# Six visits of four banks, or three of six: regrouping attention inside a fused attention and FFN kernel

## The chip, the cores and the metric

The kernel runs on one core of one Trainium2 chip. The metric is device time in microseconds (us) of that core. A run here is one execution with its own time. In an experiment the profiled execution is its first run; that of the kernel before is one more execution, of 569.2 us, at the long end of the four timed ones. A profiled span is mostly about 1.8 us shorter than the time of the same run. With a single core no second state was seen: every run with a timed comparison counted as fast. Runs without a comparison (e1, e2 and e5 to e9, one execution each) have no known state; of these I rest on the trace, and give the time for the record.

## The reference

Linformer attention over 8 batches of 8 heads, and then a gated feed-forward network (FFN) over the 8192 tokens:

```python
k_proj = np.einsum('ks,bhsd->bhkd', E, k)        # 1024 keys -> 64
v_proj = np.einsum('ks,bhsd->bhkd', F, v)
scores = scale * np.matmul(q, k_proj.transpose(0, 1, 3, 2))
attn   = np.exp(scores - max); attn = attn / (sum(attn) + 1e-09)
out    = np.matmul(attn, v_proj)                 # 64 per head
x      = out.transpose(0, 2, 1, 3).reshape(8192, 512)
gate   = 1.0 / (1.0 + np.exp(-(x @ w_gate)))     # 512 x 1536
val    = x @ w_val                               # 512 x 1536
return (gate * val @ w_out)                      # 1536 x 512
```

(The maximum and the sum are shortened here.) The FFN is most of the work: 288 matmuls of 128x128 weights on 512 columns per batch, against 56 small matmuls of attention that run side by side in parts of the array.

## The kernel before

TensorE runs the FFN of batch b in 32 steps (24 of "G and V", 8 output projections), and at fixed steps it is interrupted for a piece of the attention of batch b+1. I call such an interruption a visit. Helpers add an instruction to a plan with what it reads, writes and which PSUM bank it holds; the plan makes the semaphores. There are eight banks: four in turn for the FFN (`ffn`), four for attention (`att`).

One FFN step and its gate, which hold two banks:

```python
def mstep(blk, m):
    pbs = {n: ffn.next() for n in "GV"}
    for n in "GV":
        for i in range(NI):                    # 4 matmuls each
            mm_one(blk, m, i, n, pbs[n])       # 128x128 weights, 512 columns
    gate(blk, m, pbs["G"], pbs["V"])           # ScalarE tanh -> sig, VectorE (sig+1)*V -> hT
```

The attention of batches 2 to 7 (cut to its core):

```python
def kv():                                      # 16 matmuls in pairs, tiles 128*64, one bank
    ...                                        # then ScalarE: bank -> kpd, vpD
def turn_kd(): ...                             # DMA transpose kpd -> kpD
def sc(r2):                                    # tiles 64*64
    for r in (2 * r2, 2 * r2 + 1):
        bks = [att.next(), att.next()]
        ...                                    # 4 matmuls kpD, qT -> two banks
        ...                                    # ScalarE exp -> eT, frees the banks
def den():                                     # 8 matmuls in fours, tiles 128*32, one bank
    ...
    for c in range(4):
        rec(c, bk)                             # VectorE reciprocal, 128 columns each
def gather(): ...                              # DMA rden -> rrow
def spread(rnd): ...                           # GpSimd partition_broadcast rrow -> rb
def xo(r2):                                    # tiles 64*64
    for r in (2 * r2, 2 * r2 + 1):
        bks = [att.next(), att.next()]
        ...                                    # 4 matmuls vpD, eT -> two banks
        for g in range(2):                     # VectorE: bank * rb -> xT, frees the bank
            dve(... tensor_tensor(xT[...], bank[...], rb[...], ALU.mult) ...)

return [kv, turn_kd, lambda: sc(0), lambda: sc(1), den, gather,
        lambda: spread(0), lambda: spread(1), lambda: xo(0), lambda: xo(1)]
# at steps
spots = (3, 6, 10, 13, 16, 16, 20, 23, 26, 29)
```

So six of these pieces are visits of TensorE: projection, two of scores, denominators, two of outputs. Batch 1 has its own list, with the division spread by matmul: four reciprocals, a split of the result into two bf16 parts (`split`: a copy to `rhi`, the rest to `rhl`), and broadcast matmuls on `rhl` (`bc`). Batch 0 comes first of all, in two halves, while the loads arrive; I call the time until the FFN runs without gaps the head. In it, idle time of TensorE is filled with dummy matmuls (`busy(n)`), and GpSimd issues the loads, one after the other, each costing it some 0.8 to 1.0 us.

The softmax here doesn't subtract the row's maximum and nothing guards it: scores larger than these inputs give would overflow.

## Time and profile before

| | before |
|---|---|
| median of all its runs beside the change | 568.76 us (567.77 to 569.41, 4 runs) |
| profiled span | 567.4 us |
| TensorE busy | 97% |
| FFN matmuls without a gap, each | 0.2158 us |
| attention visits of batches 2 to 7 | 36, each 0.23 us beside its matmuls |
| period per batch | 67.41 us |

How to read the profile: "PE" is TensorE, "PEld" its weight loads, DVE VectorE, ACT ScalarE, POOL GpSimd. A line of the timeline has start, duration, engine, line of the program, operation, what it writes and reads, shapes, and how many instructions are merged; in brackets the idle time before it and who ended it. The durations of matmuls include their way through the array, so I never add them: what a stretch costs is read from the starts on both sides of it.

VectorE's timeline in the head, where the first half of batch 0 is divided:

```profile
16.94 0.95 DVE L593 RECIPROCAL rden<-pF 64x128 f32<-64x128 f32 x1 [0.55 <-PE pF L220]
17.92 0.22 DVE L594 CAST rhi<-rden 64x128 bf16<-64x128 f32 x1
...
18.94 0.96 DVE L593 RECIPROCAL rden<-pA 64x128 f32<-64x128 f32 x1 [0.42 <-PE pA L220]
19.93 0.62 DVE L594 CAST rhi<-rden 64x128 bf16<-64x128 f32 x1
```

GpSimd's timeline, the issue of a load for the second batch:

```profile
19.48 1.02 POOL L238 DMA_DIRECT2D KV<-in_v_dram  x1
```

The view of one tile, `rb`, the broadcast reciprocals: minimum, median and maximum duration in ns, and first and last start.

```profile
L829 POOL PARTITION_BROADCAST rb<-rrow x96: 792/797/802, 130.4 to 479.2; - x96
L854 DVE TENSOR_TENSOR xT<-pA,rb x56: 680/681/684, 81.9 to 489.8; 128x512 bf16<-128x512 f32 x56
```

In the kernel before, broadcasts and multiplies are regular to within 10 ns.

### The profile page before, as it was taken

How to read it: one execution, taken by the hardware profiler on the slowest of the kernel's cores; microseconds unless marked ns; L12 is line 12 of the kernel's file. 1: busy time of each engine (PE TensorE's matmuls, PEld its weight loads, DVE VectorE, ACT ScalarE, POOL GpSimd, SP SyncE). 2: the span in 40 equal slices, each digit the busy share in tenths (PEclk: the TensorE clock that was granted, in tenths of full speed). 3: DMA queues.
4: the chain of work that ended last, by engine and by line, in shares of the span. 5: the costliest groups of instructions: out<-in, count | busy, mean ns of one | idle time of the engine just before them, and what ended most of it. 6: DMA issues, size and time to landing. Idle time of an engine off the chain costs nothing.

```text
span 567.4 us, 7629 instructions
## 1 busy us (share of the span) xinstructions
PE 550.5 (97%) x2963; PEld 247.0 (44%) x3018; DVE 249.5 (44%) x397; ACT 177.4 (31%) x314; POOL 107.2 (19%) x148
## 2 busy tenths in 40 slices
PE   5899999999999999999999999999999999999998
PEld 4444434444444444444444444444444444444444
DVE  4544464353623545235443256334462354633332
ACT  2644632432143322352223422243214332222220
POOL 9400201007200080002600054000700007000000
PEclk9999999999999999999999999999999999999999
DMA  9999999936944059512677046560601001010112
GB/s 162 198 201 201 140 212 167 208 79 115 146 84 96 21 113 183 93 47 62 117 141 121 24 105 107 121 103 37 114 18 48 37 22 39 37 37 20 38 38 92
DMA packets 76564, 56.00 MB, mean 99 GB/s; under 512 B 34704, under 2 KB 68240, under 8 KB 76528
## 3 DMA queue, kind: packets, MB, share of 16 engines
q0 software_dynamic: 33984, 29.89, 34.8%
q1 hardware_dynamic: 42544, 25.63, 18.1%
q8 instruction: 23, 0.38, 0.3%
q14 instruction: 13, 0.11, 0.1%
HBM read 60.29 MB, written 16.78 MB: 136 GB/s over the span
## 4 chain that ended last, share of the span: by engine, by line
PE 95%; DVE 1%; DMA 1%; issue 1%; ACT 0%; POOL 0%; DVEq 0%; POOLq 0%
PE pF L220 88%; PE pA L220 7%; DMA KV<-in_k_dram 1%; DVE xT L645 1%; DVE hT L940 0%; DVE rden L783 0%; DVE rhl L794 0%; ACT qT L224 0%; DVE rhi L792 0%; POOL quad L313 0%; DVE ost L971 0%; DVEq L102 0%; POOLq L1116 0%
## 5 line engine op out<-in xcount | busy, mean ns | idle before, releaser
L940 DVE SCALAR_TENSOR_TENSOR hT<-sig,pF 128x512 bf16<-128x512 f32 x192 | 130.8, 685 | 200.0 <-PE pF L220 145.1
L224 ACT ACTIVATE sig<-pF 128x512 f32<-128x512 f32 x192 | 114.4, 599 | 318.3 <-PE pF L220 315.9
L220 PE MATMUL pF<-xT,wV 128*128 128x512 bf16 x753 | 196.2, 379 | 1.1 <-DVE hT L940 0.3
L220 PE MATMUL pF<-xT,wG 128*128 128x512 bf16 x746 | 194.4, 379 | 2.8 <-issue 1.3
L220 PE MATMUL pF<-wO,hT 128*128 128x512 bf16 (+2 forms) x762 | 173.9, 376 | 1.5 <-issue 0.8
L220 PEld LDWEIGHTS pF<-wO,hT 128*128 128x128 bf16 x780 | 74.7, 98 | 92.6 <-issue 6.2
L220 PEld LDWEIGHTS pF<-xT,wV 128*128 128x128 bf16 x768 | 75.1, 98 | 91.1 <-DVE hT L940 0.8
L220 PEld LDWEIGHTS pF<-xT,wG 128*128 128x128 bf16 x768 | 72.2, 98 | 95.3 <-issue 12.3
L829 POOL PARTITION_BROADCAST rb<-rrow x96 | 70.7, 798 | 217.1 <-DMA rrow<-rden 212.0
L971 DVE TENSOR_SCALAR ost<-pF 128x512 f32<-128x512 f32 (+1 forms) x65 | 44.4, 684 | 103.5 <-PE pF L220 103.4
L224 ACT ACTIVATE eT<-pA 128x512 bf16<-128x512 f32 x63 | 32.7, 606 | 8.4 <-PE pA L220 8.4
L854 DVE TENSOR_TENSOR xT<-pA,rb 128x512 bf16<-128x512 f32 x56 | 34.7, 682 | 0.0
L783 DVE RECIPROCAL rden<-pA 128x128 f32<-128x128 f32 x28 | 24.1, 916 | 0.0
L238 POOL DMA_DIRECT2D KV<-in_v_dram x9 | 7.8, 872 | 83.9 <-PE pF L220 83.9
L220 PE MATMUL pA<-KV,EFT 128*64 128x512 bf16 (+2 forms) x168 | 16.0, 332 | 1.0 <-DMA KV<-in_k_dram 1.0
L224 ACT ACTIVATE kpd<-pA 64x1024 bf16<-64x1024 f32 x6 | 6.1, 1017 | 28.3 <-PE pA L220 28.3
L238 POOL DMA_DIRECT2D KV<-in_k_dram x9 | 8.0, 889 | 32.3 <-PE pF L220 32.2
L220 PEld LDWEIGHTS pA<-KV,EFT 128*64 128x64 bf16 x168 | 8.3, 115 | 8.6 <-issue 3.4
L224 ACT ACTIVATE vpD<-pA 64x512 bf16<-64x512 f32 (+2 forms) x22 | 10.2, 465 | 2.2 <-PE pA L220 1.7
L220 PE MATMUL pA<-qT,kpD 64*64 64x512 bf16 (+1 forms) x140 | 10.4, 367 | 0.0
L220 PE MATMUL pA<-eT,vpD 64*64 64x512 bf16 (+1 forms) x140 | 10.4, 367 | 0.0
L238 POOL DMA_DIRECT2D Qb<-in_q_dram x11 | 9.4, 865 | 0.0
(69 smaller groups left out, 89.5 us busy)
## 6 DMA issues: line engine op xcount, KB each, us to landing
out_dram<-ost SPq DMA_DIRECT2D x63, 256.0 KB, 2.1
Qb<-in_q_dram POOLq DMA_DIRECT2D x7, 1024.0 KB, 15.6
KV<-in_k_dram POOLq DMA_DIRECT2D x7, 1024.0 KB, 11.0
KV<-in_v_dram POOLq DMA_DIRECT2D x7, 1024.0 KB, 10.5
wO<-in_moe_w_out_dram POOLq DMA_DIRECT2D x1, 1536.0 KB, 12.0
wG<-in_moe_w_gate_dram POOLq DMA_DIRECT2D x5, 256.0 KB, 18.4
wV<-in_moe_w_val_dram POOLq DMA_DIRECT2D x5, 256.0 KB, 19.0
KV<-in_k_dram POOLq DMA_DIRECT2D x2, 512.0 KB, 8.8
```

Of the source, the lines that this page charges most:

```text
L220: return add("PE", lambda e: e.matmul(o, lhsT, rhs, **kw), r=r, x=[("bank", b)])
L224: return add("ACT", lambda e: e.activation(o, i, func, scale=scale), r=r, w=w, x=x)
L238: add("POOL", lambda e: e.dma_start(o, i), r=r, w=w, dma=sem)
L645: lambda e, g=g, o=o: e.tensor_tensor(o, bank[bks[g]][:, :].rearrange("p (r c) -> p r c", r=2), rb[:, 2 * R + g, :].rearrange("p (r c) -> ...
L783: lambda e: e.reciprocal(rden[:, cc], bank[bk][:, cc]),
L829: lambda e, n=n, i=2 * rnd + c, j=j, parts=parts: e.partition_broadcast(rb[0:parts, n, :], rrow[32 * j : 32 * j + 1, i, :], channels=parts),
L854: lambda e, r=r, g=g, n=n, bk=bks[g]: e.tensor_tensor(xT[s][:, r, :, 256 * g : 256 * g + 256], bank[bk][:, :].rearrange("p (f c) -> p f c" ...
L940: lambda e: e.scalar_tensor_tensor(hT[blk % 2][:, m, :], sg[:, :], 1.0, bank[pv][:, :], ALU.add, ALU.mult,),
L971: lambda e, pb=pb, c0=c0, c1=c1: e.tensor_scalar(o[:, c0:c1], bank[pb][:, 0 : c1 - c0], 0.5, None, op0=ALU.mult),
```

## The change

The intent: fewer interruptions of the FFN. A visit may hold six banks, four of attention and two borrowed from the FFN. So that the outputs' banks come free without waiting for the division, ScalarE copies them unscaled to SBUF (`xu`), and VectorE multiplies from there later. The third visit also projects the next batch's keys and values and forms the denominators. The core of the diff, cut:

```diff
-        Qb = [sbuf(f"Qb{i}", [P, H, S // P * DH], BF16) for i in range(2)]
+        Qb = sbuf("Qb", [P, H, S // P * DH], BF16)
...
+        xu = sbuf("xu", [P, 8, 512], FP32)
...
+            def scores():
+                f, a0, a1 = two(ffn), two(att), two(att)
+                for r, bks in ((2, f), (0, a0), (1, a1)):
+                    sc_one(r, bks)
+                exp_one(2, f)
+                exp_one(0, a0)
+                held["sc"] = a1
+
+            def mixed():
+                f, a0, a1 = two(ffn), two(att), two(att)
+                sc_one(3, f)
+                xo_one(0, a0)
+                xo_one(1, a1)
+                exp_one(3, f)
+                keep_x(0, a0)
+                held["x"] = a1
+
+            def outputs():
+                f, a0 = two(ffn), two(att)
+                xo_one(2, f)
+                xo_one(3, a0)
+                held["x"] = a0
+                if b + 1 < B:
+                    held["kv"] = att.next()
+                    kv(b + 1, held["kv"])
+                den()
+                keep_x(2, f)
+                rec(0)
...
-                spots = (3, 6, 10, 13, 16, 16, 20, 23, 26, 29)
+                spots = (3, 4, 6, 7, 12, 13, 14, 15, 15, 21, 23, 25, 27)
```

The second batch keeps its pieces, but their order and steps change:

```diff
-                    v_alone,
                     lambda: sc(0),
                     lambda: sc(1),
...
+                    v_alone,
+                    lambda: rec(3),
                     split,
...
-                spots = (12, 13, 14, 15, 16, 17, 18, 19, 20, 20, 21, 22, 23, 24)
+                spots = (12, 13, 14, 15, 16, 17, 18, 18, 19, 19, 21, 22, 23, 24)
```

Not shown: batch 2 has its own projection visit and its own steps, and the loads of the later batches are issued at other steps, with the queries last. And in the head there are more fillers, scores before denominators, another order of banks, and the loads of the second batch are written later:

```diff
-        busy(6)
+        busy(18)
...
-        den(0)
         sc(1)
+        den(0)
...
-        load_q(1)
-        load_k(1)
-        load_v(1)
+        def second_loads():
+            load_q(1)
+            load_k(1)
+            load_v(1)
...
+                put(5, second_loads)
```

## The prediction

> **What bounds the kernel now**
>
> I read the page first: engine shares, then the chain that ended last.
>
> ```profile
> PE 550.5 (97%) x2963; PEld 247.0 (44%) x3018; DVE 249.5 (44%) x397; ACT 177.4 (31%) x314; POOL 107.2 (19%) x148
> ...
> PE 95%; DVE 1%; DMA 1%; issue 1%; ACT 0%; POOL 0%; DVEq 0%; POOLq 0%
> ```
>
> TensorE is busy for 97% of the span and carries 95% of the chain; no other engine passes 44%. So only what shortens TensorE's own stream, or one of its few waits, can count. A busy share hides what lies between instructions, so next I read the TensorE timeline of the steady part, start by start.
>
> ```profile
> 230.29 1.92 PE L220 MATMUL pA<-KV,EFT 128*64 128x512 bf16 x16
> ...
> 289.84 1.03 PE L220 MATMUL pF<-xT,wG 128*128 128x512 bf16 x4
> ...
> 295.02 2.75 PE L220 MATMUL pF<-wO,hT 128*128 128x512 bf16 x12
> 297.70 1.92 PE L220 MATMUL pA<-KV,EFT 128*64 128x512 bf16 x16
> ```
>
> From 289.84 to 295.02 lie 24 feed-forward (FFN) matmuls without a gap: 5.18/24 = 0.2158 us each. Key projections follow each other at 67.41 us: that is one batch. Its FFN is 288 matmuls, 288 x 0.2158 = 62.15 us, so attention costs 5.26 us of TensorE per batch. The small attention matmuls run side by side in parts of the array, in "rounds" that cost one matmul's time: 8 rounds of projection (16 matmuls in pairs), 4 of scores, 2 of denominators, 4 of outputs: 18 x 0.2158 = 3.88 us. The other 1.38 us is what six interruptions of the FFN ("visits") cost: 0.23 us each. One visit seen directly:
>
> ```profile
> 311.65 1.03 PE L220 MATMUL pF<-xT,wV 128*128 128x512 bf16 x4
> 312.61 0.63 PE L220 MATMUL pA<-qT,kpD 64*64 64x512 bf16 x8
> 313.17 2.76 PE L220 MATMUL pF<-wO,hT 128*128 128x512 bf16 x12
> ```
>
> 311.65 + 4 x 0.2158 = 312.51, so the visit enters 0.10 us late; its two rounds end at 313.04 and the FFN resumes at 313.17, another 0.13. Nothing waits for an engine here: the price belongs to the change of tiling (128*128 to 64*64 and back).
>
> Then I looked for real waits of TensorE. The largest is in the second batch's attention:
>
> ```profile
> 72.88 1.03 PE L220 MATMUL pF<-xT,wV 128*128 128x512 bf16 x4
> 75.15 0.39 PE L220 MATMUL pA<-rhl,bsel 32*128 32x512 bf16 x4 [1.24 <-DVE rhl L794]
> ```
>
> 72.88 + 0.86 + 0.10 = 73.84 is when the visit could start; it starts 1.31 us later. The VectorE timeline says why:
>
> ```profile
> 72.89 0.95 DVE L783 RECIPROCAL rden<-pA 128x128 f32<-128x128 f32 x1
> 73.88 0.43 DVE L792 CAST rhi<-rden 128x512 bf16<-128x512 f32 x1
> 74.34 0.75 DVE L794 SCALAR_TENSOR_TENSOR rhl<-rhi,rows,rden 128x512 bf16<-128x512 bf16 x1
> ```
>
> The last reciprocal and the split sit in the very step before the broadcast needs them. Last, the head, from the same TensorE timeline:
>
> ```profile
> 9.35 1.06 PE L220 MATMUL pA<-KV,EFT 128*64 128x128 bf16 x16 [1.01 <-DMA KV<-in_k_dram]
> ...
> 13.24 1.03 PE L220 MATMUL pA<-ident,Qb 128*128 128x128 bf16 x8
> 14.21 0.30 PE L220 MATMUL pF<-ident,kp 128*64 128x128 bf16 x4
> ...
> 15.20 0.40 PE L220 MATMUL pA<-ident,Qb 128*128 128x128 bf16 x4
> 15.44 0.39 PE L220 MATMUL pF<-ident,Qb 128*128 128x128 bf16 x4
> ```
>
> Eight transposes take 0.97 us at 13.24 (0.12 each) and four take 0.24 at 15.20 (0.06 each): the array runs at half speed until about 14.5. But the arrival of data also paces it. Issue times plus times to landing give 11.8 for the second half of the keys, 13.2 and 14.5 for the queries, 17.0 and 19.7 for the values; each piece of TensorE work starts close behind its landing. The first FFN matmul is at 22.62.
>
> **What the Trainium skill says**
>
> "TensorEngine Tiling (Array Packing)", Key Properties: changing the tiling mode, not just the tile, drains TensorE. The trace agrees: 0.10 + 0.13 us per visit.
>
> "TensorE: Matmul & The Clock Gate", What's actually happening: the array runs at half clock until some 3.4 us of sustained work. The 0.12 and 0.06 us above agree.
>
> "VectorE: DVE Perf Modes", TRN2 errata: an fp32 tensor_tensor with SBUF operands takes (N+151)/0.96, 691 ns at 512. The trace has 682 ns for the present multiply, which reads PSUM, so the multiply's new source should cost nothing.
>
> "SBUF — State Buffer", Who interferes with whom: a VectorE instruction with two SBUF inputs contends with a GpSimd instruction that reads SBUF. The new multiply is one and the partition broadcast the other. No such overlap exists in the kernel before.
>
> **The change, part by part**
>
> *Visits.* The kernel before makes 6 x 6 = 36 visits for batches 2 to 7. The new one makes 18, and one more for batch 2's own key and value projection: 19. The rounds stay 18 per batch. Saved: 17 x 0.23 = 3.9 us. The third visit, however, changes tiling inside: 64*64 for outputs, 128*64 for the next projection, 128*32 for denominators. That is two inner changes for five batches and one for the last, 11 in all. Their size I take from the head, where projection changes straight to denominators:
>
> ```profile
> 17.92 0.22 PE L220 MATMUL pF<-KV,EFT 128*64 128x128 bf16 x1
> 18.07 0.83 PE L220 MATMUL pA<-eT,dsel 128*32 128x128 bf16 x8
> ```
>
> 17.92 + 0.05 for that matmul leaves 0.10 us. 11 x 0.10 = 1.1 us is given back: net -2.8 us.
>
> *Second batch.* The denominators move one step earlier and the value projection between the reciprocals, so about two more FFN steps of 1.73 us lie between split and broadcast. The 1.31 us wait should vanish: -1.3 us. The visits there stay ten.
>
> *Head.* More filler matmuls warm the array before the keys land; 18 cold ones (some 1.9 us from 7.5) may delay the first projection by 0.1 us, while later transposes and projections halve. The landings above cap the gain. Following VectorE, the first reciprocal stays at about 16.9, but the second need no longer wait 0.42 us for TensorE, so the first scaled outputs and the FFN start move up 0.4 to 0.5 us. I count -0.45.
>
> *Off the path.* ScalarE takes 8 more evictions per batch, 6 x 8 x 0.5 = 24 us over the run at 31% busy. VectorE's multiplies only change source. One query buffer instead of two makes the second batch's query load wait for the last transposes of the first, near 34.6; the weights ahead of it occupy the queue until the last lands at 17.0 + 21.4 = 38.4, so it arrives no later (43.4).
>
> Sum: -2.8 - 1.3 - 0.45 = -4.55. 568.17 - 4.55 = **563.6 us**.
>
> **Rivals**
>
> *Bank waits.* Each visit now borrows two of the FFN's four banks. The tightest place is the second visit after two FFN steps. Count from the first visit: its exponentials start 0.5 us in and four take 2.06, so the next tanh ends near 3.1 us; two more exponentials; the tanh after them ends near 4.6, and the gate on VectorE (0.69) frees the bank near 5.4. The second visit needs it at about 6.15. Slack 0.75 us: no wait, but it is the thinnest point. If ScalarE ran later by 1 us, six batches would lose some 0.3 us each, and the time would be about 565.5.
>
> *VectorE against GpSimd.* Broadcasts take 12.7 us per batch and start 10.3 us after the third visit; the first two multiplies (17 and 22 us after it) may overlap them. Each VectorE instruction could lose up to one broadcast, 0.8 us. Gates would slip by 1 to 2 us; the output projection beside them gives slack. I expect at most some tenths per batch; the bad case is 566.
>
> *Inner changes cost nothing, or double.* Nothing: 562.5. A full 0.23 each: 565.0.
>
> *The freed time is lost to loads.* Against it: TensorE waits for no load after 10 us, and the new loads are issued earlier.
>
> **Range and chances**
>
> The visit count and the 1.31 us wait are firm; inner changes, head and bank slack each move the sum by about a microsecond, mostly upward. 562.0 to 566.0 should hold it 8 times in 10. A 2% gain needs 11.4 us, more than all visits and stalls named here: 0.01. A 2% loss needs a wait of about 2 us in every batch: 0.01. Within 2%: 0.98.
>
> **What would show it**
>
> In the new TensorE timeline: period per batch of 62.15 + 3.88 + 3 x 0.23 + 0.2 = 66.9 us against 67.41; no wait for the split near 73 us; first FFN matmul near 22.2. Inner gaps of 0.1 between the three tilings. Wrong would be FFN matmuls marked as waiting for ACT eT, DVE hT or DVE xT after a visit, multiplies well over 0.69 us, or a broadcast over 0.8 us.

## The result, and the profile after

| | before | after |
|---|---|---|
| median | 568.76 us | 564.57 us (564.34 to 564.6, 4 runs) |
| profiled span | 567.4 us | 562.8 us |
| third FFN step starts | 26.66 us | 25.89 us |
| first broadcast matmul of batch 1 | 75.15 us | 73.07 us |
| period per batch | 67.41 us | 66.97 us |

The ratio of the times is 0.9927, with a 95% interval of 0.9909 to 0.9945. A ratio here is the mean time of one kernel's fast runs over that of the other's of the same rounds, so not quite the ratio of the medians. The change is worth 0.7%, within the 2% that counts as the same.

From the page of the kernel after, the engines' shares and the chain of work that ended last:

```profile
PE 551.9 (98%) x3032; PEld 248.8 (44%) x3032; DVE 258.5 (46%) x397; ACT 200.8 (36%) x362; POOL 113.0 (20%) x148
...
PE 96%; DMA 2%; DVE 1%; POOL 0%; issue 0%; ACT 0%; POOLq 0%
```

TensorE was the bound before and still is. ScalarE's 48 new copies made it 23 us busier, from 177.4 to 200.8, and VectorE went from 249.5 to 258.5 with as many instructions as before.

The TensorE timeline after, at the first visits of two batches and at one third visit:

```profile
162.31 0.41 PE L221 MATMUL pF<-qT,kpD 64*64 64x512 bf16 x4
...
180.38 1.03 PE L221 MATMUL pF<-xT,wV 128*128 128x512 bf16 x4
181.34 0.41 PE L221 MATMUL pF<-eT,vpD 64*64 64x512 bf16 x4
181.57 0.39 PE L221 MATMUL pA<-eT,vpD 64*64 64x512 bf16 x4
181.89 1.92 PE L221 MATMUL pA<-KV,EFT 128*64 128x512 bf16 x16
183.74 0.61 PE L221 MATMUL pA<-eT,dsel 128*32 128x512 bf16 x8
184.29 1.04 PE L221 MATMUL pF<-xT,wG 128*128 128x512 bf16 x4
...
229.28 0.41 PE L221 MATMUL pF<-qT,kpD 64*64 64x512 bf16 x4
```

The period is 229.28 - 162.31 = 66.97. In the third visit, the last FFN matmul gives way at 180.38 + 0.86 = 181.24; the visit starts 0.10 later. Four matmuls of 64*64 cost one round, two rounds would end at 181.34 + 0.43 = 181.77; the projection starts at 181.89, 0.12 later. Its eight rounds end at 183.62; the denominators start 0.12 later. Their two rounds end at 184.17, and the FFN resumes 0.12 later. Other third visits of the trace give 0.12 to 0.13 for each inner change. I use 0.125.

The broadcast matmuls of batch 1, where the kernel before waited 1.24 us:

```profile
72.11 1.03 PE L221 MATMUL pF<-xT,wV 128*128 128x512 bf16 x4
73.07 0.39 PE L221 MATMUL pA<-rhl,bsel 32*128 32x512 bf16 x4
```

72.11 + 0.86 + 0.10 = 73.07: no wait at all.

VectorE's and GpSimd's timelines in the head of the kernel after, which answer to those shown of before:

```profile
16.96 0.95 DVE L593 RECIPROCAL rden<-pF 64x128 f32<-64x128 f32 x1 [0.86 <-PE pF L221]
17.94 0.22 DVE L594 CAST rhi<-rden 64x128 bf16<-64x128 f32 x1
...
18.57 0.96 DVE L593 RECIPROCAL rden<-pA 64x128 f32<-64x128 f32 x1
19.57 0.23 DVE L594 CAST rhi<-rden 64x128 bf16<-64x128 f32 x1
```

```profile
17.00 0.87 POOL L239 DMA_DIRECT2D wV<-in_moe_w_val_dram  x1
```

The second reciprocal no longer waits (18.57 against 18.94, with the same start of the first), the second copy takes 0.23 us and not 0.62, and the load shown is GpSimd's last before the copies are done.

The view of tile `rb` after:

```profile
L831 POOL PARTITION_BROADCAST rb<-rrow x96: 792/797/1210, 137.1 to 473.0; - x96
L862 DVE TENSOR_TENSOR xT<-xu,rb x48: 678/684/1153, 143.2 to 481.2; 128x512 bf16<-128x512 f32 x48
```

Some multiplies and some broadcasts take half as long again or more: the contention that the prediction named as a rival, and two of its signs of being wrong. On the page the multiplies' mean went from 682 to 856 ns.

Three stretches make up the gain between these two traces. Until the third FFN step: 26.66 - 25.89 = 0.77. From there to the broadcast matmuls: 75.15 - 73.07 = 2.08 in all, so 1.31. From there to the end: 567.4 - 562.8 = 4.6 in all, so 2.5.

The theory at this point: fewer visits save 2.5, the vanished wait 1.31, a better head about 0.8. The rivals: that the head's share is chance, since loads land differently from run to run; that the gap of a visit belongs to interruption as such and not to the change of tiling; that the contention or the banks cost something that hides in the sum.

### The profile page after: what moved, and what is told of

It reads as the page before. It is cut to its first block, busy times and chain, and to the rows that moved or that the text cites. A ratio compares the mean times of both kernels' runs of the same rounds, so it can differ in the third digit from the quotient of the medians.

```text
span 562.8 us, 7706 instructions
## 1 busy us (share of the span) xinstructions
PE 551.9 (98%) x3032; PEld 248.8 (44%) x3032; DVE 258.5 (46%) x397; ACT 200.8 (36%) x362; POOL 113.0 (20%) x148
## 4 chain that ended last, share of the span: by engine, by line
PE 96%; DMA 2%; DVE 1%; POOL 0%; issue 0%; ACT 0%; POOLq 0%
PE pF L221 90%; PE pA L221 6%; DMA Qb<-in_q_dram 2%; DVE xT L645 1%; POOL KV L239 0%; DVE hT L992 0%; DVE rden L593 0%; ACT qT L225 0%; POOL quad L313 0%; DVE rhl L596 0%; DVE ost L1023 0%; DVE rhi L594 0%; POOLq L1179 0%
## 5 line engine op out<-in xcount | busy, mean ns | idle before, releaser
L221 PE MATMUL pF<-xT,wG 128*128 128x512 bf16 x768 | 198.0, 379 | 1.2 <-DVE xT L645 1.2
L221 PE MATMUL pF<-wO,hT 128*128 128x512 bf16 (+1 forms) x780 | 175.7, 376 | 0.0
L831 POOL PARTITION_BROADCAST rb<-rrow x96 | 77.0, 862 | 286.3 <-DMA rrow<-rden 281.1
L862 DVE TENSOR_TENSOR xT<-xu,rb 128x512 bf16<-128x512 f32 x48 | 39.2, 856 | 0.0
L785 DVE RECIPROCAL rden<-pA 128x128 f32<-128x128 f32 x28 | 26.6, 951 | 12.3 <-PE pA L221 12.3
L225 ACT ACTIVATE eT<-pA 128x512 bf16<-128x512 f32 x39 | 21.3, 626 | 1.6 <-PE pA L221 1.6
L225 ACT ACTIVATE eT<-pF 128x512 bf16<-128x512 f32 x25 | 13.6, 595 | 22.6 <-PE pF L221 22.4
L225 ACT ACTIVATE xu<-pA 128x512 f32<-128x512 f32 x36 | 19.1, 617 | 0.0
L225 ACT ACTIVATE rb<-pA 128x512 f32<-128x512 f32 x14 | 7.4, 601 | 2.1 <-PE pA L221 2.1
```

Of the source, the lines that this page charges most:

```text
L221: return add("PE", lambda e: e.matmul(o, lhsT, rhs, **kw), r=r, x=[("bank", b)])
L225: return add("ACT", lambda e: e.activation(o, i, func, scale=scale), r=r, w=w, x=x)
L785: lambda e: e.reciprocal(rden[:, cc], bank[bk][:, cc]),
L831: lambda e, n=n, i=2 * rnd + c, j=j, parts=parts: e.partition_broadcast(rb[0:parts, n, :], rrow[32 * j : 32 * j + 1, i, :], channels=parts),
L862: lambda e, r=r, g=g, n=n, x=x: e.tensor_tensor(xT[s][:, r, :, 256 * g : 256 * g + 256], x.rearrange("p (f c) -> p f c", f=2), rb[:, n, :] ...
```

## The experiments

There were twelve runs of kernels. e1 to e4 were on one chip, e5 to e8 on a second, e9 and e10 on the first again, e11 and e12 on a third, each time with runs of the kernel before (a single one beside e5 to e8). All twelve gave correct results.

### One part at a time

**The late loads alone** (e1), on the kernel before:

```diff
-        load_q(1)
-        load_k(1)
-        load_v(1)
+        def second_loads():
+            load_q(1)
+            load_k(1)
+            load_v(1)
...
+                put(5, second_loads)
```

> The kernel before with one edit: the loads of the second batch (queries, keys, values, output weights) are issued after the sixth FFN step, as in the changed kernel, instead of ahead of the FFN. In the kernel before, the copy that splits the second reciprocal ran 0.62 us from 19.93 while GpSimd issued the value load (19.48 to 20.50); in the changed kernel it ran 0.23 us. Theory 'loads': GpSimd's issue work slows that copy, so here the copy takes about 0.23 us and the first FFN matmul moves from 22.62 to about 22.2; the steady FFN from 26.66 to about 26.3. Rival 'order and fillers': the copy was slow for another reason; it stays near 0.6 and the first FFN matmul stays at 22.6. The end of the span should move by the same 0.3 to 0.4 us or not at all.

Measured: 569.22 us, span 567.4. The experiment failed. The loads were written later, but each engine has its own order, GpSimd had nothing in between, and nothing made the loads wait: in the trace they are issued at 17.73, 18.61 and 19.47, as before. In the kernel after, they wait because the single query buffer must be free. So this run is a repeat of the kernel before. It is of use as such: here the two copies take 0.70 and 0.34 us, where the kernel before had 0.22 and 0.62.

**The head alone** (e2): fillers, order and banks of the kernel after, on the kernel before; the loads stay early.

```diff
-        busy(6)
+        busy(18)
...
-        den(0)
         sc(1)
+        den(0)
```

> The kernel before with the head of the changed kernel alone: more filler matmuls, second scores ahead of the first denominators, the new turn of banks; the loads stay early. Theory 'loads plus order': of the 0.77 us that the changed kernel gains by its third FFN step, order and fillers give about 0.4 (the second reciprocal starts near 18.57 instead of 18.94), and the copy stays slow at about 0.6 us: third FFN step near 26.3 instead of 26.66. Rival 'order and fillers alone': the whole 0.77, 25.9.

Measured: 568.32 us, span 566.5. The third FFN step starts at 25.79, the copies take 0.22 and 0.25, and the wait of batch 1 is still there (1.24 us at 74.27). By its place alone this third FFN step says little, since e3 below reaches 25.78 with the old head; the count from the first reciprocal, under "The head", shows that order and fillers shorten the head even with early loads.

**The second batch alone** (e3), on the kernel before, 5 rounds:

```diff
-                    v_alone,
                     lambda: sc(0),
...
+                    v_alone,
                     lambda: rec(3),
...
-                spots = (12, 13, 14, 15, 16, 17, 18, 19, 20, 20, 21, 22, 23, 24)
+                spots = (12, 13, 14, 15, 16, 17, 18, 18, 19, 19, 21, 22, 23, 24)
```

> The kernel before with the second batch's order alone: denominators one step earlier, value projection among the reciprocals. Theory: the wait of 1.31 us ahead of the broadcast matmuls at 75.15 goes and nothing else changes: they start near 73.84, and the span is 1.3 us shorter, 0.23%: ratio to the kernel before 0.9977. Rival: the value projection, now in the same step as a reciprocal, delays something later by as much; ratio 1.000.

Measured: 567.62 us (566.39 to 568.15) against 568.42, ratio 0.9983 (0.9969 to 0.9996). TensorE's timeline:

```profile
72.00 1.03 PE L220 MATMUL pF<-xT,wV 128*128 128x512 bf16 x4
72.96 0.39 PE L220 MATMUL pA<-rhl,bsel 32*128 32x512 bf16 x4
```

The wait is gone with this part alone. A ratio of 0.9983 is 1.0 us, with an interval of 0.2 to 1.8, so the 1.31 of the trace fits. The profiled span, 565.2, is lower by 2.2 and not by 1.3: the head is code of the kernel before, yet its third FFN step starts at 25.78 instead of 26.66, because the first keys landed at another time. The head of one and the same program differs by 0.9 us between executions.

**The visits alone** (e4): the kernel after, with the head's order and the second batch of before. The loads stay late, as the single query buffer demands. 5 rounds:

```diff
-        busy(18)
+        busy(6)
...
+        den(0)
         sc(1)
-        den(0)
...
+                    v_alone,
                     lambda: sc(0),
...
-                    v_alone,
```

> The changed kernel with the head and the second batch's order of the kernel before: three visits of six banks alone (the late loads stay, as there is one query buffer). Theory: 17 visits fewer at 0.23 us (3.9) minus 11 inner changes of tiling at 0.125 (1.4) give 2.5 us; the late loads 0.4 more; so 2.9 us shorter, ratio 0.995; batch period 66.97; the 1.3 us wait near 75 is back. Rival 'the steady gain depends on the other edits': another period than 66.97.

Measured: 565.92 us (565.04 to 566.42) against 568.42, ratio 0.9953 (0.9939 to 0.9966): 2.7 us. The period is 66.97, and the wait is back:

```profile
74.91 0.39 PE L221 MATMUL pA<-rhl,bsel 32*128 32x512 bf16 x4 [1.24 <-DVE rhl L796]
```

Both copies in the head took 0.22 us here, with the old order of the head but without GpSimd's issues at that moment.

**Everything but the visits** (e12): head and second batch of after on the kernel before, six visits, early loads; 5 rounds. The edits are those of e2 and e3 together.

> The kernel before with the changed kernel's head (fillers, order, banks) and its second batch's order, with the six visits and the early loads kept: all of the change but the visits. Theory 'the parts add up': the wait ahead of the broadcast gives 1.3 us, the head 0.4 to 0.9; ratio 0.9963 to 0.997, and with the three-visit kernel's 0.9953 it makes about 0.992 (the changed kernel has 0.9927, with one part, the late loads, counted on the other side). Batch period 67.41. Rival 'the head gives nothing once the landing of the loads differs from run to run': 0.9977.

Measured: 568.04 us (566.43 to 568.23) against 569.18, ratio 0.9982 (0.9968 to 0.9997). That is 1.0 us, no more than the second batch alone gave. The trace of its fastest run has span 564.6 with everything in place: copies of 0.22 and 0.23 us, no wait of batch 1, third FFN step at 25.19. But three of its six runs had a mean granted clock of 0.997 instead of 1.0, and spans of 566.4, 566.3 and 566.4; the other three had 564.6, 566.1 and 565.2. This is taken up below. The three runs at full clock have a mean of 567.13, 1.7 us below the mean of the kernel before (568.81), but in the time of all its runs, the head's share isn't resolved. The ratios of e4 and e12 multiply to 0.9935, against 0.9927 for the whole change. The difference is some 0.5 us, less than either interval is wide.

### What a visit costs

**Denominators over the whole array** (e5), on the kernel before: 8 matmuls with full 128*128 tiles, the weights padded with zeros, in place of 8 in two rounds of four. No change of tiling, but still an interruption.

```diff
-                            bank[bk][32 * j : 32 * j + 32, :],
-                            dsel[:, n % 2, rnd, :],
+                            bank[bk][:, :],
+                            dselF[:, n, :],
                             eT[:, n, :],
...
-                            tp=(0, 32 * j),
```

> The kernel before with the denominators computed by eight matmuls over the whole 128 x 128 array (selection matrices padded with zeros) instead of eight 128 x 32 ones side by side. The visit then needs no change of tiling, but still interrupts the FFN, takes a bank from the attention's ring and reads other tensors. Theory 'tiling': the visit enters and leaves without a gap; each costs 8 x 0.2158 = 1.73 us instead of 0.66, so +1.07 us for each of seven batches, +7.5 us in all, and the batch period grows from 67.41 to 68.48. Rival 'interruption': the 0.10 us before and 0.13 us after it stay; period 68.71, +9.1 us in all.

Measured: 576.73 us against 569.18 (slower, as intended). TensorE's timeline:

```profile
192.11 1.03 PE L221 MATMUL pF<-xT,wV 128*128 128x512 bf16 x4
192.97 1.89 PE L221 MATMUL pA<-eT,dselF 128*128 128x512 bf16 x8
194.70 1.03 PE L221 MATMUL pF<-xT,wG 128*128 128x512 bf16 x4
```

192.11 + 0.86 = 192.97 and 192.97 + 8 x 0.2158 = 194.70: the visit enters and leaves without any gap. The period is 68.49 (164.75 to 233.24). Six more matmul times are 1.29, less 0.23 for the vanished gaps is 1.06; 67.41 + 1.06 = 68.47. So the 0.23 us is the price of going to another tiling and back. The interruption itself, another PSUM bank and other operands, costs nothing that can be read.

**The projection in a visit of its own** (e6), on the kernel after: four visits instead of three.

```diff
-                if b + 1 < B:
-                    held["kv"] = att.next()
-                    kv(b + 1, held["kv"])
+                held["kv"] = att.next()
...
-                lambda: (rec(2), keep_kd(held["kv"]) if b + 1 < B else None),
+                lambda: (kv(b + 1, held["kv"]) if b + 1 < B else None, rec(2), keep_kd(held["kv"]) if b + 1 < B else None),
```

> The changed kernel with the next batch's projection taken out of the third visit and given its own visit two steps later. Five batches: one visit more (0.22 to 0.23) and, inside the third visit, one change of tiling (64*64 to 128*32) instead of two (0.13 and 0.12). Theory 'an inner change costs about half a visit': +0.10 us per batch, period 67.07 instead of 66.97. Rival 'every change of tiling costs the same full visit, or inner ones are free': period 66.97 or 67.2.

Measured: 565.13 us, period 67.07 to 67.08. TensorE's timeline:

```profile
162.42 0.41 PE L221 MATMUL pF<-qT,kpD 64*64 64x512 bf16 x4
...
229.50 0.41 PE L221 MATMUL pF<-qT,kpD 64*64 64x512 bf16 x4
```

One more visit (0.23), one inner change less (0.125): 66.97 + 0.105 = 67.075. The size of the inner change is confirmed by a second arrangement.

### The rivals: contention and banks

**Multiplies later** (e7), on the kernel after:

```diff
-                spots = (3, 4, 6, 7, 12, 13, 14, 15, 15, 21, 23, 25, 27)
+                spots = (3, 4, 6, 7, 12, 13, 14, 15, 15, 24, 25, 27, 29)
```

> The changed kernel with the four pairs of multiplies moved later (from steps 21, 23, 25, 27 to 24, 25, 27, 29 of a batch), so that they start after the partition broadcasts end. In the changed kernel the multiplies from SBUF took 684 ns at the median but up to 1153, and broadcasts up to 1210 against 802 before. Theory 'VectorE and GpSimd contend, off the path': no multiply over 0.70 us and no broadcast over 0.81 in batches 3 to 7, and the period stays 66.97. Rival 'reading SBUF makes them slower by itself': slow ones stay. Rival 'they cost time': the period falls below 66.97.

Measured: 564.94 us, period 66.97. For batches 3 to 7, which the edit moves clear of the broadcasts, the 40 multiplies take 681 to 687 ns and the 80 broadcasts 792 to 801, as the view of `rb` from 155 us on shows:

```profile
L831 POOL PARTITION_BROADCAST rb<-rrow x80: 792/797/801, 194.8 to 472.7; - x80
L862 DVE TENSOR_TENSOR xT<-xu,rb x40: 681/685/687, 208.8 to 485.0; 128x512 bf16<-128x512 f32 x40
```

In batch 2, which the edit does not move, the longest are still 1148 and 1207 ns. So it is the overlap that lengthens both, as the Trainium skill's page "SBUF — State Buffer", section "Who interferes with whom", says of a VectorE instruction with two SBUF inputs. And it costs no time: with the overlap gone in five batches of six the period is the same to 0.01 us.

**One and two more copies on ScalarE** (e8 and e9), on the kernel after, placed among the exponentials of the first visit. They delay the gates and so the return of the borrowed banks.

```diff
                 exp_one(2, f)
+                for _ in range(1):     # 2 in e9
+                    act(rhi[:, :], eT[:, 4, :], [("eT", 4), ("rhi", 0)], [("rhi", 0), ("rhi", 1)])
```

> The changed kernel with one extra ScalarE copy of 128 x 512 (to a tile that nobody uses then) in the first visit of each batch, some 0.6 us. The slack of the borrowed banks was worked out as 0.75 us; in the trace of the changed kernel the gate ends at 301.51 and the second visit starts at 302.31, 0.80 us. Theory 'slack of 0.8': no wait of TensorE, period 66.97. Rival 'ScalarE already holds the second visit up': period grows by up to 0.6.

> The changed kernel with two extra ScalarE copies, one after the other, in the first visit of each batch: some 1.2 to 1.3 us. Theory 'slack of 0.8': the second visit now waits for the bank by about 0.4 to 0.5 us per batch; period about 67.4, 5 x 0.45 = 2.2 us longer than the changed kernel (the second batch has other steps and more slack). Rival 'ScalarE has room for more': period stays 66.97.

In the kernel after, the gate whose bank the second visit borrows starts at 300.82 and takes 0.69; the visit starts at 302.31. The slack is 302.31 - 301.51 = 0.80 us.

Measured with one copy: 565.96 us, period 66.97: no wait, as the copy takes 0.65 in the trace, which is below 0.80. The 1.4 us by which it is slower than the change is in the head, whose third FFN step starts at 27.25 instead of 25.89, and has to do with the clock (below).

Measured with two copies, 1.31 us together: 566.35 us, period 67.38. The weight loads of TensorE name the wait, in the middle of the second visit:

```profile
302.97 0.11 PEld L221 LDWEIGHTS pF<-qT,kpD 64*64 64x64 bf16 x3 [0.25 <-DVE hT L994]
```

`hT` is what the gates write. A delay of 1.31 us costs 0.41 per batch: the slack is real, it is about as large as predicted, and the rival of the bank wait comes true with two more ScalarE copies in the first visit, though not with one.

**The gates first** (e10), on the kernel after, 5 rounds. At the change of blocks in batch 0, TensorE waits twice in both kernels, 0.82 us together, for multiplies and gates on VectorE. This tries a better order there:

```diff
-                put(9, lambda: (xo2(0), xo2(1)))
+                put(9, lambda: (xo2(0), late.update(mul=xo2(1, False)), late["gate"]()))
```

(The parts that hold back the multiplies and the gate are left out.)

> The changed kernel with one reordering on VectorE where the first block of batch 0 ends: the gates of the last two FFN steps go between the two pairs of multiplies instead of before and after all four. In the changed kernel TensorE waits there 0.34 us (for the multiplies, at 47.05) and 0.48 us (for the gate, at 48.84). Theory 'order only': both waits go, but the last pair of multiplies now ends later and costs about 0.45 at 48.9: net 0.4 us shorter, ratio to the kernel before 0.992. Rival 'VectorE has too much work there for any order': 0.8 us of waits stay, ratio 0.9927 as the changed kernel.

Measured: 564.63 us (564.3 to 565.73) against 569.17, ratio 0.9928 (0.9916 to 0.9941), against 0.9927 for the change itself. In the trace, one wait of 0.48 us is left of the two (0.34 us less), but in time it isn't resolved.

### The head

**The loads really wait** (e11), on the kernel before, 5 rounds. What e1 meant to do:

```diff
         def load_q(b):
...
+                r=[("qT", 0, 1, R, x) for R in range(2) for x in range(2)] if b == 1 else (),
```

> The first attempt at this (the kernel before with its second loads written later in the program) turned out to leave GpSimd's own order as it was: the loads still went out at 17.7 to 20.5 us. Here the query load of the second batch waits for the last transposed queries of the first, as in the changed kernel, so all three loads go out near 34 us. Theory 'GpSimd slows the copy': both copies that split a reciprocal take 0.22 us (they took 0.22 and 0.62 in the kernel before, 0.70 and 0.34 in the first attempt, 0.22 and 0.22 in the three-visit kernel, whose loads are late), and from the first transpose of queries to the third FFN step it takes about 12.6 us, as in the three-visit kernel, instead of 13.2 to 13.4. In the time that is 0.4 to 0.8 us, ratio 0.9986 to 0.9993, close to what five rounds can resolve. Rival: the copies stay irregular, 13.2 to 13.4 stays, ratio 1.000.

Measured: 568.45 us (567.72 to 569.53) against 569.18, ratio 0.9993 (0.9978 to 1.0008): nothing resolved. The loads now leave at 34.56, 35.43 and 36.30. The copies took 0.58 and 0.23 us. I had held that GpSimd's issue of these loads lengthens the copies, so the 0.58 looked like a contradiction.

It isn't one, when all copies of all traces are set beside what GpSimd does at that moment. There are 28, two in each of 14 traces. Twenty take 0.22 or 0.23 us. The other eight:

| trace | copy starts, lasts, ends | GpSimd issue under way, its end | copy ends after it by |
|---|---|---|---|
| before | 19.93, 0.62, 20.55 | 19.48 to 20.50 | 0.05 |
| e1 | 18.09, 0.70, 18.79 | 17.73 to 18.75 | 0.04 |
| e1 | 20.20, 0.34, 20.54 | 19.47 to 20.49 | 0.05 |
| e2 | 19.43, 0.25, 19.68 | 18.61 to 19.64 | 0.04 |
| e3 | 19.15, 0.53, 19.68 | 18.61 to 19.63 | 0.05 |
| e5 | 18.02, 0.55, 18.57 | 17.47 to 18.53 | 0.04 |
| e5 | 20.04, 0.29, 20.33 | 19.21 to 20.28 | 0.05 |
| e11 | 16.59, 0.58, 17.17 | 16.26 to 17.13 | 0.04 |

Every one of them started at least 0.33 us into an issue and ended 0.04 or 0.05 after the issue's end. In e11 it was the issue of an FFN weight. The short ones started with no issue under way, or less than 0.2 us into one, or just before the end of one. So a copy that meets an issue in its later part waits until the issue is over. The same section of the Trainium skill has a rule that fits: a cast can take the port pair which VectorE shares with GpSimd, and whoever comes first keeps it while the other is blocked. That the port is the reason was not tested, and no edit here set the overlap on purpose (e11 moved the late loads away, and its first copy met another issue); that the lengthened copies end with the issues was read from every trace that has one.

With this, the head can be counted from the first reciprocal to the third FFN step, which leaves out when the data lands:

| trace | order of the head | excess of the copies over 0.22 | first reciprocal to third FFN step |
|---|---|---|---|
| e4 | old | 0, 0 | 9.32 |
| e5 | old | 0.33, 0.07 | 9.39 |
| e1 | old | 0.48, 0.12 | 9.53 |
| e3 | old | 0, 0.31 | 9.62 |
| before | old | 0, 0.40 | 9.72 |
| after, e2, e6, e7 | new | 0, at most 0.03 | 8.93 to 8.96 |
| e9, e12 | new | 0, at most 0.01 | 9.02 |
| e8, e10 | new, granted clock lowered | 0, 0.01 | 10.16, 10.04 |

An excess of the second copy counts in full: 9.32 + 0.31 = 9.63 and 9.32 + 0.40 = 9.72. An excess of the first is swallowed by the 0.42 us that the second reciprocal waits for TensorE anyway, but for the few hundredths in e1 that are left over. (e11 has 9.72 with a second copy of 0.23; there the first multiply comes 6.08 us before the third step, against 5.68 in the other old heads, as TensorE waited for the values to land: 9.72 - 0.40 = 9.32.) The new order is worth 9.32 - 8.94 = 0.38.

The last line of the table is the clock. The view by stretches of 5 us, for the kernel after and for e8 (start and end, length, then busy time and count of PE, PEld, DVE, ACT, POOL, and then granted clock, DMA share and GB/s):

```profile
20.00:25.00 5.00, 4.00 (x44) 1.76 (x43) 2.75 (x5) 2.64 (x8) 0.00 (x0) 1.00 1.45 195
```

```profile
20.00:25.00 5.00, 3.81 (x40) 1.64 (x40) 2.89 (x5) 2.53 (x7) 0.00 (x0) 0.68 1.45 195
```

In e8, whose code in the head is that of the kernel after, TensorE's granted clock falls to a mean of 0.68 in this stretch; FFN matmuls there start 0.42 us apart instead of 0.216. From 22 to 24 us the same view gives 0.50, in e8 and in e10. A mean of 0.66 or 0.68 over 5 us is thus some 3.2 to 3.4 us at half clock, an estimate from these two figures. (The view doesn't show everything: from 5 to 15 us it gives 1.00 in both kernels, where the prediction reads half speed from the spacing of the transposes. There the spacing is the evidence.) It costs some 1.1 us (10.16 or 10.04 against 8.94 to 9.02). Of the 21 runs of kernels with the new head, six had a mean granted clock of 0.997: the one of e8, two of e10, three of e12. No run with the old head had it: not the five of e4, not those of e1, e3, e5 and e11, and none of the kernel before. (One run of e11 and the one of e6 had 0.999.) What trips it isn't settled. The idle time just before the first FFN matmul doesn't decide it: it was 1.19 us in e8 and only 0.35 in e10, which both had it, and 0.81 to 1.03 in the kernel after, e6 and e7, which did not.

## Why the prediction was right

It said 563.6 us and a range of 562.0 to 566.0; the median was 564.57. The prediction started from 568.17, the median of the first three runs of the kernel before; with the fourth run it is 568.76. So the gain is better compared than the time: 4.55 predicted, 4.19 between the medians, 4.6 between the traces, of which that of before is a long execution.

- *Visits: -2.8 predicted, -2.5 measured.* 17 visits saved at 0.23, as counted. The mis-sized term is the inner change of tiling, 0.10 in the prediction and 0.125 in the trace: 11 x 0.125 = 1.4 given back instead of 1.1; 3.9 - 1.4 = 2.5. The 0.10 came from one pair of lines in the head, where the matmuls have 128 columns. The visits of the kernel before, with 512 columns, had shown 0.13 on the way out, and would have been the better source. e6 confirms 0.125, e5 that the tiling is what is paid.
- *What it said the profile would show:* a period of 66.9 (66.97), no wait near 73 us (none, at 73.07), the first FFN matmul near 22.2 (21.64), inner gaps of 0.1 (0.12 to 0.13).
- *Second batch: -1.3 predicted, -1.31 measured* in the trace of the whole change, and its disappearance again with this part alone (e3) and its return without it (e4).
- *Head: -0.45 predicted, -0.77 measured in the two traces.* The step itself, the second reciprocal no longer waiting for TensorE, gave 0.38 (traces alone; in time it isn't resolved). The other 0.40 was not in the prediction: in the traced run of the kernel before, the second copy waited for one of GpSimd's issues, and the kernel after issues nothing then. The lines were there before the change was run, two equal copies of 0.22 and 0.62 us; I took the split as a constant. It is a matter of phase, though: in other traces of the old head with early loads the same copy lost from 0.07 to 0.31, and with the loads moved away (e4, e11) nothing. Against this the new head sometimes loses 1.1 us to the clock, which no step of the prediction had; it happened in none of the four timed runs of the change. That landings cap the gain was right: with the array warm earlier, TensorE now waits 0.47 us for the first queries, at 13.37, so "TensorE waits for no load after 10 us" holds for the kernel before only.
- *Off the path:* ScalarE's 48 copies cost no time, as predicted (23 us more busy time, predicted 24), and the late query load kept nobody waiting.
- *Rival, bank waits:* slack predicted 0.75, measured 0.80; e8 and e9 put it between 0.65 and 1.31.
- *Rival, VectorE against GpSimd:* the overlap came true, with up to 1153 ns for a multiply of 684 and 1210 for a broadcast of 797. That a multiply from SBUF costs nothing thus holds only outside the overlap (681 to 687 ns in e7). The price in time is zero, not "some tenths per batch": e7 has the same period without the overlap.
- *Rival, inner changes free or at 0.23:* neither. *Rival, gain lost to loads:* not visibly; the 0.47 us above lies within the head's count.

So two misses, 0.3 too much for the visits and 0.3 too little for the head, cancelled between the two traces. The mechanism of the two largest terms was right; that their sum came out so close is luck, since half of the head's share came from a copy that the prediction had taken as a constant. What remains open: why a copy waits for an issue, what lowers the clock in the new head in some runs, and how much that costs the changed kernel in the long run. The traced gain of the head is thus that of an undisturbed run.

## What to carry to other kernels

When one engine is busy for 97% of the span, read the starts of its instructions and not its busy share: gaps of a tenth of a microsecond between tilings, 36 times over, were the largest thing left. Merge work by tiling mode, but count the changes inside a merged visit too, since each costs half of what the visit saves. Before calling a wait hidden or a duration constant, look whether equal instructions have equal durations in the trace; where they don't, look at what the other engine was doing and where that ended.

## What the Trainium skill lacked or had wrong

- "TensorEngine Tiling (Array Packing)", Key Properties: it says that a change of tiling mode drains TensorE, but gives no figure. Here 128*128 to a smaller tile and back costs 0.10 us in and 0.12 to 0.13 us out, a change between 64*64, 128*64 and 128*32 costs 0.12 to 0.13 us at 512 columns, and an interruption without change of mode costs nothing (0.00 in e5).
- "SBUF — State Buffer", Who interferes with whom: it says that the second to come is blocked, which would cover this case, but of GpSimd's DMA issues it names only the other direction, that VectorE can starve them. Here it was VectorE's copy that lost: it (64x128, 0.22 us) took up to 0.70 us and ended 0.04 to 0.05 us after the issue, in all eight cases that were at least 0.33 us into one, and was not lengthened in the first 0.2 us of an issue. For multiply against broadcast both sides were lengthened (up to 1153 ns from 684, up to 1210 from 797).
- "TensorE: Matmul & The Clock Gate", What's actually happening: it has the clock fall back after an idle window of some 3.4 us. Here it fell to a mean of 0.66 to 0.68 over 5 us in the head of two traces, with no idle time of TensorE above 1.2 us in the 8 us before it. The page's section "A second HAM failure mode: psum-queue depth-cycling" does have frequent short idles lower the clock; whether that is the case here was not tested.
- "TensorE: Matmul & The Clock Gate", Back-to-back issue gap: its figure of some 131 ns per matmul at 512 columns in a stream with weight loads isn't seen here. In that stream the spacing is 0.2158 us, which is what the same section gives for a single isolated matmul.
